# Delta attention and a PReLU feed-forward layer on one core: issuing loads of the first weight behind the first chunk's chain of small products

## The chip, the cores and the metric

The kernel runs on one core of one Trainium2 chip. The metric is the device time of one execution in microseconds (us), lower is better. The core has a matrix engine (TensorE, PE in the profile; PEld is its weight load), a vector engine (VectorE, DVE), a scalar engine (ScalarE, ACT), GpSimd (POOL) and SyncE (SP), which in this kernel issues nearly all transfers. Each engine works through its own list of instructions in order, and waits for other engines by semaphores.

## The reference

A gated delta-rule attention over 4 batches, 8 heads, 768 positions and head size 48, followed by a feed-forward layer from 384 to 2048 and back:

```python
for t in range(S):
    kt, vt, bt = (k_n[:, :, t], v[:, :, t], beta[:, :, t, None])
    y[:, :, t] = np.einsum('bhd,bhde->bhe', q[:, :, t], state)
    v_old = np.einsum('bhde,bhd->bhe', state, kt)
    state = state + bt[:, :, :, None] * np.einsum('bhd,bhe->bhde', kt, vt - v_old)
...
x = np.ascontiguousarray(attn_out.transpose(0, 2, 1, 3)).reshape(B * S, H * D)
...
h = x @ w_in
g = np.maximum(h, 0.0) + alpha * np.minimum(h, 0.0)
return (g @ w_out).astype(np.float32)
```

`k_n` is k divided by its norm. The feed-forward input has 3072 rows. The two weights are the reason for this case: they lie in memory as 64-bit numbers, and the kernel makes 32-bit numbers of them itself.

## The kernel before, in words

**Tiling.** The sequence is cut into 12 chunks of 64 positions, and the batch into two pairs, so there are 24 steps, `n` = 0 to 23. Steps 0 and 1 are the two pairs of chunk 0, steps 2 and 3 those of chunk 1, and so on. Within a chunk the recurrence is turned into a triangular system: its inverse is built by VectorE for blocks of 32 (`eliminate`, `eliminate_small`, `cross`), put together by many small products (`between_1`, `between_2`), applied to v (`solve`), and used for the output (`outputs`) and for the next state (`next_state`). `to_ffn` transposes the output of a step into `xt`, the input of the feed-forward layer. `ffn_in(c)` multiplies it with `w_in` (48 products for a chunk, six to a PSUM bank, two banks by turns), and ScalarE and VectorE empty a bank with one Relu (L913) and two VectorE instructions (L915).

**Order.** The order is written by hand; a generator is advanced for every instruction or two, and `weave` and `alongside` mix several generators in fixed proportions. What is written first goes first into each engine's list. Nothing is moved later by a scheduler.

**The weights.** `weights` returns three things: `fetch(n)`, which issues the loads up to the n-th piece on SyncE (L192); `begin(n)`, which does the first two of four conversion steps on ScalarE (L208, L209); and a generator `finish`, which does the other two on VectorE (L218, L223) and, after each piece, issues the loads of all further pieces whose staging buffer has come free (L227 to L230). `w_in` has 12 pieces of 512 KB each, numbered 0 to 11 here. There are `n_in` = 6 staging buffers, which lie in the space that `w_out` will take, so pieces 0 to 5 are loaded at the start, and piece 6 can be loaded only once piece 0 has been converted, piece 7 once piece 1 has, and so on. `ahead` says how far ScalarE's two steps may run ahead of VectorE's.

**Around the change.** `first_chunk` carries steps 0 and 1 through. While it runs, no other work is ready for TensorE, and so `busy` puts products without use between the small ones. `convert(2)` converts one piece, `convert(4)` two. The order in `first_chunk` is: piece 0; then `place`, `between_1` (L676), `between_2` (L695), `solve` (L762), `outputs` (L775), pieces 1 and 2, `next_state` (L791), pieces 3 and 4; then for both steps `to_ffn`, `load_late(i + 2)` and `load_v(i + 3)`; last, piece 5. `load_late` issues four loads of 48 KB on SyncE (L144) into a buffer that the `next_state` of the step two before has to be done with. `load_v` issues two loads of 96 KB (L120).

With piece 5 the generator calls `begin(7)`, so ScalarE's list holds the two steps of piece 6 right behind the copies of `to_ffn`. `second_pair` comes next: it starts chunk 1 and weaves into it the 48 products of `ffn_in(0)` and the conversion of pieces 6 to 11. In ScalarE's list stand there, in this order: piece 6, a square of k (L330), piece 7, the two copies of `cross` (L581), two copies of `flips` (L381, L383), a square, piece 8, and the first L913.

In SyncE's list before the change stand: the load of piece 6 (behind piece 0's conversion); the loads of pieces 7, 8, 9 and 10, each behind one conversion; the 12 loads of `load_late` and `load_v`; and the load of piece 11.

Of the kernel before, what the change touches and what calls it, by code (L numbers as in the profile page):

```python
# [41 lines left out]
def kernel(  # L42
# [34 lines left out]
    def ps_one():  # L77
        return ps_big()[:, 0]
# [4 lines left out]
    def ps_ffn():  # L83
        turn[0] ^= 1
        return ffn_banks[turn[0]]

    def half(i):
        return slice(64 * i, 64 * i + 64)
# [27 lines left out]
    def fetch(a, n, dst, queues=(nc.sync, nc.sync)):  # L116
        c, bp = steps[n]
        for t in range(2):
            src = a[2 * bp + t, :, c * C : (c + 1) * C, :].rearrange("h p d -> p h d")
            queues[t].dma_start(out=dst[half(t)], in_=src)  # L120
# [9 lines left out]
    def load_v(n):  # L130
        if n < N:
            v_raw[n] = work.tile([128, H, D], FP32, name="v_raw", bufs=3)
            fetch(v, n, v_raw[n])
# [26 lines left out]
    w_in = const.tile([128, KT, DFF], FP32, name="w_in")  # L160
    w_out = const.tile([128, FT, DM], FP32, name="w_out")

    ahead = [0]

    def weights(pieces, stages, ids, done):

        count = len(pieces)
        fetched, begun = [], []

        def words(i):
            w = stages[ids[i]]
            dst, src = pieces[i]  # L180
            shape = list(dst.shape)
            n = shape[1] * (shape[2] if len(shape) > 2 else 1)
            w = w[:, 0 : 2 * n]
            if len(shape) > 2:
                return w.rearrange("p (f e) -> p f e", f=shape[1]), n
            return w, n

        def fetch(n):
            while len(fetched) < min(n, count):
                i = len(fetched)  # L190
                assert ids[i] not in ids[len(done) : i]
                nc.sync.dma_start(out=words(i)[0], in_=pieces[i][1].bitcast(U32))  # L192
                fetched.append(i)

        def flat(x):
            return x.rearrange("p f d -> p (f d)") if len(x.shape) > 2 else x

        def halves(i):
            w = flat(words(i)[0]).rearrange("p (e w) -> p e w", w=2)
            return w[:, :, 0], w[:, :, 1], flat(pieces[i][0])  # L200

        def begin(n):
            while len(begun) < min(n, count):
                i = len(begun)
                assert i < len(fetched)
                lo, hi, dst = halves(i)

                nc.scalar.activation(dst.bitcast(U32), lo, ACT.Copy, scale=2.0**-29)  # L208
                nc.scalar.activation(  # L209
                    lo.bitcast(FP32), hi.bitcast(FP32), ACT.Prelu, scale=2.0**-112, alpha=-(2.0**32)  # L210
                )
                begun.append(i)

        def finish():
            for i in range(count):
                begin(min(i + 2, max(ahead[0], i + 1)))
                lo, _, dst = halves(i)
                nc.vector.tensor_scalar(  # L218
                    out=lo, in0=lo, scalar1=3, scalar2=None, op0=ALU.logical_shift_left
                )  # L220
                yield

                nc.vector.tensor_tensor(  # L223
                    out=dst.bitcast(U32), in0=lo, in1=dst.bitcast(U32), op=ALU.add
                )
                done.append(i)
                n = len(fetched)  # L227
                while n < count and ids[n] not in ids[i + 1 : n]:
                    n += 1
                    fetch(n)  # L230
                yield

        return fetch, begin, finish()

# [154 lines left out]
    def now(pieces):  # L391
        for x in pieces:
            x()
# [171 lines left out]
    def cross(m, bs, edge, half_way, aside=None):  # L565


        def let(b, every):
            if aside is not None and b % every == every - 1:
                aside()  # L570

        n = bs.stop - bs.start
        p = ps_one()[:, 0 : n * LB].rearrange("p (b i) -> p b i", i=LB)
        for b in range(n):
            for i in range(4):
                nc.tensor.matmul(
                    p[quad(i), b], edge[quad(i), bs.start + b],
                    turned[m][quad(i), bs.start + b, 0:LB],
                )
            let(b, 4)  # L580
        nc.scalar.copy(half_way[:, bs, 0:LB], p)  # L581
        yield
        p = ps_big()[:, :, 0 : n * LB].rearrange("p w (b i) -> p w b i", i=LB)
        for b in range(n):
            for i in (0, 2):
                nc.tensor.matmul(
                    p[quad(i), 1, b], inverse[m][quad(i), bs.start + b],
                    half_way[quad(i), bs.start + b, 0:LB],
                )
            let(b, 8)  # L590
        for b in range(n):
            for i in range(4):
                nc.tensor.matmul(
                    p[quad(i), 0, b], half_way[quad(i), bs.start + b],
                    inverse[m][quad(i), bs.start + b, LB:HB],
                )
            let(b, 4)
        for i in (0, 2):
            y = turned[m][quad(i), bs, 0:LB]
            nc.vector.tensor_tensor(out=y, in0=y, in1=p[quad(i), 1], op=ALU.add)  # L600
        y = inverse[m][:, bs, LB:HB]
        nc.vector.tensor_tensor(out=y, in0=y, in1=p[:, 0], op=ALU.add)
        yield
# [7 lines left out]
    def place(n, parts=(0, 1, 2, 3), by_vector=False):  # L611
        for _ in placing(n, parts, by_vector):
            pass
# [101 lines left out]
    def scale_v(n):  # L715
        if n < N and n not in nv:
            nv[n] = v_raw.pop(n)
            nc.vector.tensor_tensor(
                out=nv[n], in0=nv[n],
                in1=stats[n][0][:, :, None].to_broadcast([128, H, D]), op=ALU.mult,  # L720
            )
# [295 lines left out]
    in_done, out_done = [], []  # L1017
# [98 lines left out]
    def busy(n, p=None):  # L1116

        p = ps_one() if p is None else p
        while n > 0:
            x = p[:, 0 : int(512 * min(n, 1))]  # L1120
            nc.tensor.matmul(  # L1121
                x, ident[0:ROWS],
                k_t[NJ - 1].rearrange("p g i -> p (g i)")[0:ROWS, 0 : x.shape[-1]],
            )
            n -= 1
# [21 lines left out]
    def first_chunk(mask, convert):  # L1147

        both = (0, 1)
        ahead[0] = n_in  # L1150

        waits, pause = iter([0.5] * 2), []
        middle = cross(
            0, slice(0, 2 * H), edge, half_way, lambda: pause and busy(next(waits, 0), pause[0])
        )
        next(middle)
        pause.append(ps_one())
        busy(1, pause[0])
        begin_in(6)
        for i in both:  # L1160
            scale_v(i)
            mask(i)
        convert(2)
        next(middle)
        busy(1.25)
        place(0, (0,))
        place(1, (0,), True)
        for i in both:
            place(i, (1,), True)
            now(between_1(i))  # L1170
        busy(0.5, ps_ffn())
        for i in both:
            place(i, (2,))
            now(between_2(i))
        for i in both:
            now(through_state(i))
            now(solve(i))
        busy(0.5, ps_ffn())
        now(outputs(0))
        convert(4)  # L1180
        now(next_state(0))
        now(outputs(1))
        now(next_state(1))
        convert(4)
        busy(0.5, ps_ffn())
        for i in both:
            to_ffn(i, ps_ffn())
            load_late(i + 2)
            load_v(i + 3)
        ahead[0] = FT * DM  # L1190
        convert(2)

    def statics(first, last):
# [18 lines left out]
    pieces = [  # L1212
        (w_in[:, i, o : o + W_IN_P], moe_w_in[i * 128 : (i + 1) * 128, o : o + W_IN_P])
        for o in range(0, DFF, W_IN_P)
        for i in range(KT)
    ]
    n = 2 * W_IN_P
    n_in = FT * DM // n
    ids = [i % n_in for i in range(len(pieces))]
    fetch_in, begin_in, conv_in = weights(  # L1220
        pieces, [space[:, i * n : (i + 1) * n] for i in range(n_in)], ids, in_done
    )
    PARTS_IN = 2 * len(pieces)

    pieces = [(w_out[:, f], moe_w_out[f * 128 : (f + 1) * 128]) for f in range(FT)]
    stages = [space_out[:, i] for i in range(SPACES)]
    for f in range(FT // 2, FT, 2):
        stages.append(w_out[:, f : f + 2].rearrange("p f d -> p (f d)").bitcast(U32))
    ids = [0, 1, 2, 3, 4, 5, 6, 0, 1, 2, 6, 0, 1, 2, 0, 1]
    fetch_out, _, conv_out = weights(pieces, stages, ids, out_done)  # L1230
    PARTS_OUT = 2 * len(pieces)

    def chain(*gens):
# [35 lines left out]
    n = 12  # L1269

    def convert(n):
        for _ in part(conv_in, n):
            pass
# [218 lines left out]
```

## Time and profile before

| What | us |
|---|---|
| Time, median of 3 runs | 678.72 |
| Lowest and highest | 677.28, 832.73 |
| The profiled run | 677.22 |
| Span in the profile | 675.5 |

| Engine | Busy, us | Share |
|---|---|---|
| TensorE, products | 650.6 | 96% |
| TensorE, weight loads | 567.3 | 84% |
| VectorE | 452.1 | 67% |
| ScalarE | 271.4 | 40% |
| GpSimd | 35.9 | 5% |

The share of TensorE is that of the whole span. The change lies in the first 60 us of it, which have other limits: there the slices of the page show TensorE, VectorE, ScalarE and the transfers all far from a steady state. So the table tells only that time lost or gained by TensorE in the early part is not made up later by a large reserve; what the change does has to be read from the stretch from 34 to 70 us.

The transfers of that stretch are of three kinds: pieces of the weights (512 KB in packets of 4096 bytes), q, k and v (48 or 96 KB in packets of 192 bytes), and TensorE's own instructions, which the page lists as q8 "instruction": 74 packets, 1.21 MB in all.

### The profile page before, as it was taken

What the parts mean: (1) busy time and instruction counts of PE and PEld (TensorE: products, weight loads), DVE (VectorE), ACT (ScalarE), POOL (GpSimd) and SP (SyncE); (2) the same over time, 40 slices, a digit from 0 to 9 for tenths busy, and PEclk for the clock granted to TensorE, in tenths of its full rate; (3) what the DMA queues carried; (4) which work ended last, traced back from release to release, by engine and by line L of the source; (5) the groups of instructions that cost most, each with busy time, mean ns of one, the idle gap of its engine ahead of it and who ended that gap; (6) DMA issues with size and microseconds to landing.
All of it is one profiled execution on the core that took longest, in us unless ns stands there. A gap on an engine that the chain in (4) does not pass through costs nothing.

```text
span 675.5 us, 21591 instructions
## 1 busy us (share of the span) xinstructions
PE 650.6 (96%) x9359; PEld 567.3 (84%) x9359; DVE 452.1 (67%) x1125; ACT 271.4 (40%) x643; POOL 35.9 (5%) x105
## 2 busy tenths in 40 slices
PE   5999988999998999999999999999999999999997
PEld 4578877656587998998998998988989989989997
DVE  4946878878989869758859748859655355354261
ACT  4927746335556343344343343343244144021110
POOL 6000111101010000001000000000000000000000
PEclk9979999999999999999999999999999999999999
DMA  8838844211332022122112111111121110100000
GB/s 121 239 77 231 207 104 118 71 30 31 70 76 48 14 61 49 25 49 50 25 37 36 27 37 37 26 40 33 25 47 27 36 37 2 34 4 2 24 1 24
DMA packets 110959, 37.69 MB, mean 56 GB/s; under 512 B 104160, under 2 KB 107248, under 8 KB 110864
## 3 DMA queue, kind: packets, MB, share of 16 engines
q1 hardware_dynamic: 109088, 35.81, 24.5%
q8 instruction: 74, 1.21, 0.7%
q10 hardware_dynamic: 1776, 0.49, 0.4%
q14 instruction: 21, 0.17, 0.1%
HBM read 31.56 MB, written 4.72 MB: 54 GB/s over the span
## 4 chain that ended last, share of the span: by engine, by line
PE 76%; DVE 14%; ACT 5%; issue 2%; DMA 1%; SPq 1%; POOL 0%; ACTq 0%; DVEq 0%; POOLq 0%
PE p_ffn L903 30%; PE p_ffn L967 28%; DVE prod L499 2%; DVE block L505 2%; PE p_big L360 2%; PE p_big L762 2%; PE p_big L732 2%; PE p_big L775 2%; DVE act L915 2%; PE p_big L1121 2%; ACT diag L631 1%; PE p_big L407 1%; PE p_big L737 1%; PE p_big L791 1%; DVE block L472 1%
## 5 line engine op out<-in xcount | busy, mean ns | idle before, releaser
L903 PE MATMUL p_ffn<-xt,w_in 128*128 128x256 f32 x1152 | 261.6, 382 | 6.9 <-ACT sums L913 1.8
L903 PEld LDWEIGHTS p_ffn<-xt,w_in 128*128 128x128 f32 x1152 | 214.4, 190 | 38.6 <-issue 4.2
L915 DVE SCALAR_TENSOR_TENSOR act<-act,al_t,p_ffn 128x256 f32<-128x256 f32 x176 | 76.5, 476 | 81.0 <-ACT act L913 80.9
L913 ACT ACTIVATE act<-p_ffn 128x512 f32<-128x512 f32 x88 | 52.4, 595 | 144.8 <-PE p_ffn L903 144.6
L967 PE MATMUL p_ffn<-w_out,act 128*128 128x192 f32 x480 | 82.4, 328 | 0.1
L967 PEld LDWEIGHTS p_ffn<-w_out,act 128*128 128x128 f32 x480 | 77.6, 190 | 1.0 <-issue 0.5
L505 DVE TENSOR_TENSOR block<-block,prod 128x30 f32<-128x30 f32 (+9 forms) x150 | 49.9, 333 | 5.1
L499 DVE TENSOR_TENSOR prod<-block 128x30 f32<-128x30 f32 (+9 forms) x150 | 48.9, 326 | 3.3 <-POOL block L489 1.6
L987 DVE TENSOR_TENSOR o_sb<-u,p_ffn 128x192 f32<-128x192 f32 x40 | 13.3, 353 | 50.3 <-PE p_ffn L967 41.9
L816 ACT COPY xt<-p_big 128x384 f32<-128x384 f32 x22 | 10.4, 477 | 74.2 <-PE p_big L814 74.2
L967 PE MATMUL p_ffn<-space_out,sums 128*128 128x192 f32 x160 | 29.4, 327 | 0.0
L967 PE MATMUL p_ffn<-more,sums 128*128 128x192 f32 x160 | 29.3, 326 | 0.0
L755 ACT COPY y<-p_big 128x384 f32<-128x384 f32 x22 | 10.4, 477 | 43.0 <-PE p_big L737 41.3
L967 PE MATMUL p_ffn<-w_out,sums 128*128 128x192 f32 x160 | 27.6, 326 | 0.0
L967 PEld LDWEIGHTS p_ffn<-more,sums 128*128 128x128 f32 x160 | 26.6, 190 | 0.0
L967 PEld LDWEIGHTS p_ffn<-space_out,sums 128*128 128x128 f32 x160 | 26.5, 190 | 0.1
L967 PEld LDWEIGHTS p_ffn<-w_out,sums 128*128 128x128 f32 x160 | 26.3, 190 | 0.0
L708 ACT COPY inv<-p_big 32x256 f32<-32x256 f32 x38 | 13.8, 363 | 29.7 <-DVE u L766 29.4
L631 ACT ACTIVATE diag<-inverse,which 64x128 f32<-64x128 f32 (+2 forms) x60 | 24.3, 405 | 2.3 <-DVE inverse L472 1.3
L747 DVE TENSOR_TENSOR r<-v_raw,p_big 64x192 f32<-64x192 f32 (+1 forms) x66 | 23.2, 352 | 1.0
L349 POOL TENSOR_TENSOR beta_t<-beta_t,rec 128x8 f32<-128x8 f32 x24 | 6.2, 259 | 291.9 <-DVE rec L347 271.6
L332 DVE TENSOR_REDUCE norm<-ksq 128x8 f32<-128x384 f32 x24 | 13.0, 546 | 13.0 <-ACT ksq L330 13.0
(161 smaller groups left out, 954.0 us busy)
## 6 DMA issues: line engine op xcount, KB each, us to landing
w_out<-in_moe_w_in_dram SPq DMA_DIRECT2D x12, 512.0 KB, 4.9
qp<-in_q_dram SPq DMA_DIRECT2D x48, 96.0 KB, 3.0
v_raw<-in_v_dram SPq DMA_DIRECT2D x48, 96.0 KB, 2.9
kl<-in_k_dram SPq DMA_DIRECT2D x96, 48.0 KB, 2.7
out_dram<-o_sb SPq DMA_DIRECT2D x92, 48.0 KB, 1.6
space_out<-in_moe_w_out_dram SPq DMA_DIRECT2D x11, 384.0 KB, 4.6
ke<-in_k_dram SPq DMA_DIRECT2D x43, 96.0 KB, 3.1
w_out<-in_moe_w_out_dram SPq DMA_DIRECT2D x5, 384.0 KB, 4.3
```

The lines of the kernel that those rows point to most:

```text
L360: nc.tensor.transpose(p[0:ROWS, g * 128 : (g + 1) * 128], src[:, 2 * g : 2 * g + 2].rearrange("p h d -> p (h d)")[:, 0:ROWS], ident,)
L499: nc.vector.tensor_tensor(out=prod, in0=r[:, 0:j, j : j + 1].to_broadcast([128, j, n]), in1=r[:, j : j + 1, j + 1 : HB].to_broadcast([128, ...
L505: nc.vector.tensor_tensor(out=r[:, 0:j, j + 1 : HB], in0=r[:, 0:j, j + 1 : HB], in1=prod, op=ALU.add)
L631: nc.scalar.mul(out, x, which[rows, i : i + 1])
L708: nc.scalar.copy(to[rows], p[rows])
L732: nc.tensor.matmul(p[half(t ^ a), a, g], k_t[n][dims(a), g, half(t)], beside[bp][dims(a), t, g])
L747: nc.vector.tensor_tensor(out=r[to, a], in0=v_in[to, a], in1=p[own, a, :, 0:D], op=ALU.subtract)
L762: nc.tensor.matmul(p[half(t ^ a), a, g], inv[n % NE][half(t), a * G + g], rhs_[n][half(t), a, g])
L903: nc.tensor.matmul(p_h[:, i], w_in[:, t, (f + i) * 128 : (f + i + 1) * 128], xt[:, t], start=(t == 0), stop=(t == KT - 1),)
L913: nc.scalar.activation(g, p_h, ACT.Relu, scale=-1.0)
L915: nc.vector.scalar_tensor_tensor(out=g[:, i], in0=g[:, i], scalar=al_t[:, f + i : f + i + 1], in1=p_h[:, i], op0=ALU.mult, op1=ALU.add,)
L967: nc.tensor.matmul(p, x(i), w(i), start=(i == 0), stop=(i == FP - 1))
```

## The change

A flag `hold` is set at the beginning of `first_chunk`. While it is set, the conversion of a piece no longer issues the load of the next one. The loop that issued them is made a function of its own, `follow`, which is called once behind the 12 loads of `load_late` and `load_v` and in front of piece 5's conversion. So pieces 6 to 10 are loaded then, one behind the other, and piece 11 after piece 5 as before. The arithmetic, the buffers and the order on every engine except SyncE stay as they were. The aim is that the loads of `w_in` don't run beside the chain of small products.

```diff
-    ahead = [0]
+    ahead, hold = [0], [False]
...
                 done.append(i)
-                n = len(fetched)
-                while n < count and ids[n] not in ids[i + 1 : n]:
-                    n += 1
-                    fetch(n)
+                if not hold[0]:
+                    follow()
                 yield
...
-        return fetch, begin, finish()
+        def follow():
+            n = len(fetched)
+            while n < count and ids[n] not in ids[len(done) : n]:
+                n += 1
+                fetch(n)
+
+        return fetch, begin, finish(), follow
...
         ahead[0] = n_in
+        hold[0] = True
...
             to_ffn(i, ps_ffn())
             load_late(i + 2)
             load_v(i + 3)
+        hold[0] = False
+        follow_in()
         ahead[0] = FT * DM
         convert(2)
...
-    fetch_in, begin_in, conv_in = weights(
+    fetch_in, begin_in, conv_in, follow_in = weights(
...
-    fetch_out, _, conv_out = weights(pieces, stages, ids, out_done)
+    fetch_out, _, conv_out, _ = weights(pieces, stages, ids, out_done)
```

## The prediction

> **What bounds the kernel now.** I read the page first, then the chain of waits in order of time around the change, then a table of short stretches for the granted clock, then the lists of SyncE and ScalarE in order of time.
>
> The page says 96% for TensorE over the span. Nothing of the change touches TensorE's work, so the question is where TensorE waits or runs slowly near the change. The chain of waits from 36 to 58 us (start, duration, what):
>
> ```profile
> 36.74 1.11 PE p_big L676 x30
> 37.85 0.80 issue
> 38.65 1.25 PE p_big L676 x34
> 39.90 1.15 PE p_ffn L1121 x2
> 41.05 3.45 PE p_big L695 x62
> ...
> 44.60 1.73 PE p_big L762 x62
> 46.34 0.81 PE p_ffn L1121 x2
> ...
> 55.52 2.16 PE p_ffn L903 x10
> 57.68 0.33 PE p_big L586 x14
> ```
>
> TensorE itself carries the first chunk. Two things are odd: a stop of 0.80 us in the midst of L676 for which no engine is to blame, and L695, whose 64 products take 3.5 us, where 32 of them take 1.12 us in chunk 1. The table of stretches (the last three columns are granted clock, transfers' share, GB/s) tells why:
>
> ```profile
> 38.00:39.00 1.00, 0.35 (x10) 0.35 (x11) 0.00 (x0) 0.01 (x1) 0.00 (x0) 1.00 0.46 184
> 39.00:40.00 1.00, 1.00 (x32) 0.96 (x29) 0.00 (x0) 0.42 (x2) 0.00 (x0) 0.92 0.11 29
> 40.00:41.00 1.00, 1.00 (x4) 0.35 (x4) 0.00 (x0) 1.00 (x3) 0.00 (x0) 0.50 0.00 0
> ...
> 46.00:47.00 1.00, 1.00 (x16) 0.65 (x9) 0.70 (x3) 0.00 (x0) 0.00 (x0) 0.67 0.00 0
> ```
>
> From 39.84 to 46.67 the clock is half. The reader is also to see the zeros at the right: no transfer runs in these slow microseconds. Of the loads that the change moves, only piece 6 lies beside the chain. SyncE's list shows it, and then the others:
>
> ```profile
> 34.98 17.57 SPq L192 DMA_DIRECT2D w_out<-in_moe_w_in_dram  x5
> 52.65 2.65 SPq L144 DMA_DIRECT2D kl<-in_k_dram  x4
> 55.35 1.84 SPq L120 DMA_DIRECT2D v_raw<-in_v_dram  x2
> 57.29 2.63 SPq L144 DMA_DIRECT2D kl<-in_k_dram  x4
> 59.98 1.61 SPq L120 DMA_DIRECT2D v_raw<-in_v_dram  x2
> 61.71 0.54 SPq L192 DMA_DIRECT2D w_out<-in_moe_w_in_dram  x1
> ```
>
> The five in the first line, looked at singly, start at 34.98, 48.10, 49.17, 51.16 and 52.23. Last, who uses them. ScalarE's list (idle before an instruction in brackets) has piece 6 at 50.90, piece 7 at 52.62 and the two copies (L581) on which TensorE's L586 depends behind both:
>
> ```profile
> 50.90 0.69 ACT L208 ACTIVATE w_in<-w_out 128x512 uint32<-128x512 uint32 x1
> 51.62 0.69 ACT L209 ACTIVATE w_out<-w_out 128x512 f32<-128x512 f32 x1
> ...
> 52.62 0.69 ACT L208 ACTIVATE w_in<-w_out 128x512 uint32<-128x512 uint32 x1
> 53.34 0.70 ACT L209 ACTIVATE w_out<-w_out 128x512 f32<-128x512 f32 x1
> 53.92 0.25 ACT L581 COPY act<-p_big 128x128 f32<-128x128 f32 x1
> 54.62 0.27 ACT L581 COPY act<-p_big 128x128 f32<-128x128 f32 x1 [0.45 <-PE p_big L576]
> ```
>
> So ScalarE starts piece 6 as soon as the copies of `to_ffn` are through.
>
> [...] So a load behind a waiting load waits too; SyncE's 12.5 us wait for piece 1's conversion ahead of 48.10 agrees.
>
> **The change part by part.**
>
> *Piece 6 leaves the chain.* Its packets of 4096 bytes run from 36.30 to 39.6. [...] until 36.3 the transfers are packets of 192 bytes of q, issued from 31.78 to 34.88, which stay. So piece 6 can lengthen only what lies between the block's last byte and TensorE's going on: 36.86 to 38.65, 1.8 us. At the two other stops of this kind (85.95 and 89.74) that gap was 1.46 and 1.25 us. With 1.25 the stop shrinks from 0.80 to 0.25; bounds 0 and 0.8. I take 0.25. Then L676 ends at 39.2[...]. From 36.3 to 39.2 there are 2.9 us without a dense product[...], where before there were 3.5. So the dip probably goes, though not surely: other windows (101.3 to 104.7) keep the full clock with 1.8 us idle and 1.6 us of dense products, but no trace shows where the limit lies.
>
> *What the dip costs.* At full clock: L676 to 39.2, L1121 0.63 to 39.8, L695 64 products as 2 x 1.1 to 42.05, L703 0.42 and the second half of L762 0.54 with the latencies to 43.15, L1121 0.63 to 43.8. Before, L775 began at 47.07. Gain 3.3 us if the dip goes, about 0.5 if it stays.
>
> *Pieces 7 to 10 and piece 6 go behind 12 loads.* The first of the 12 needs `next_state(0)`, whose products end at 48.2 before, 44.9 with the gain. The page's and the lists' price of an issue is 0.65 us (2.65 for 4, 1.29 for 2): 12 make 7.8. So piece 6 is issued at 44.9 + 7.8 = 52.7. From issue to landing the pieces took 4.4 to 5.5, median 4.5 in this stretch: 57.2. Piece 7 comes 1.5 us later (512 KB at 340 GB/s), and so on. Their issue costs SyncE nothing that counts; the k and v loads now come some 4 to 5 us earlier, and nobody waits for them.
>
> *The wait that this adds.* ScalarE would start piece 6 at 50.9 - 3.3 = 47.6; now it stands until 57.2, 9.6 us. Queued behind it are the square, piece 7, L581, L381, L383, a square, piece 8 and the first L913. TensorE can do without them all up to L586: two groups of six `ffn_in` products fill two banks, of which nine products are reached, and `cross` and `flips` have buffers. It reaches L586 at 57.68 - 3.3 = 54.4. ScalarE: 57.2, pieces 6 and 7 2.8, square 0.45, first L581 0.25: 60.75. TensorE waits 6.3 us there. Against before, L586 comes at 60.8 instead of 57.7, 3.1 later.
>
> *What follows.* ScalarE has L581, L381, L383, square and piece 8 to do before L913: 0.25 + 0.5 + 0.48 + 0.42 + 1.3 gives 63.7, L913 0.55, L915 twice 0.87: 65.1. Only then may the last of the next four products use its bank; it ends at 65.35, where before they ended at 61.5: 3.8 later. [...] the clock halves once more. Until it comes back (two windows, 6.8 us, going by the first dip) TensorE loses up to 3.4, of which most lies beside ScalarE's catching up; I take 1. Sum: -3.3 + 7.1 + 1.0 = 4.8 us slower. From 58 to 90 us TensorE is busy over 90% of the time, so this isn't given back; ScalarE's idle pieces there (1.09, 1.69, 1.48, 1.11) let it catch up, not TensorE.
>
> **The rivals.**
>
> *A, the dip stays.* [...] Then +7.1 + 1.0 - 0.5 = 7.6: 685.6.
>
> *B, faster: the loads are hidden anyway.* For it: before, ScalarE waits only 0.4 us for a load anywhere from 10 to 130 us, by the list of waits, ScalarE is busy 40% only, and pieces may land sooner with no other loads in flight. Against: the list puts piece 6 behind 7.8 us of issues, and ScalarE takes it first. If ScalarE's wait cost TensorE nothing, 678 - 3.3 = 674.7; over 2% faster isn't reached even so, and would need something that no view shows.
>
> *C, the delay grows:* the issues take 8.9 us as before, landing takes 9.7 (the longest of `w_in`)[...], and the clock stays half for longer. 10 + 4 us: 692 or more. Nothing in the trace makes all of it likely.
>
> **How the numbers follow.** The base is 678 (677.28 and 678.72 of three runs; 832.73 is out of line). Forecast, dip gone and the wait paid: 678 + 4.8, about 682.8; chance 0.42. A: 685.6, 0.30. B: 674.7, 0.16, of which 0.03 for over 2% faster. C: 0.12. Two per cent is 13.6 us, so the forecast and A and nearly all of B are within it: faster 0.03, same 0.85, slower 0.12. The range from 676 to 690 takes in the forecast with the bounds of its costs, A, and half of B; what is left out is C and the lower half of B, about 0.2.
>
> **What would show it.** In the profile after: no load of 512 KB between 35 and 52 us; the 12 small loads from about 45; piece 6 issued near 53. The granted clock 1.00 from 40 to 47, L695 in about 2.2 us, the stop in L676 under 0.4: right on the gain; a half clock there means A. ScalarE idle for 8 us or more ahead of L208, released by a transfer, and TensorE idle for 5 us or more ahead of L586, with a dip behind it: right on the wait. If ScalarE's idle time there is under 3 us, or TensorE isn't held at L586, the main step is wrong.

## The result, and the profile after

The changed kernel takes 682.87 us (median of 6 runs, 681.88 to 685.04) against 677.68 for the kernel before (median of 6). The ratio is 1.0092, with an interval of 1.0063 to 1.0122: slower by 0.9%. One of the 6 runs of before, of 832.73 us, lies far above the other five (674.53 to 678.72) and says nothing of the kernel. On another occasion the same kernel came to 687.94 against 675.32, ratio 1.0171 (1.0135 to 1.0207). The experiment g1_change_again below takes up why the two differ.

The chain of waits of the changed kernel, from the first small products to the point where TensorE goes on with chunk 1 (start, duration, what; L680, L699, L766, L779 and L590 are L676, L695, L762, L775 and L586 of before):

```profile
37.50 2.24 PE p_big L680 x64
39.74 0.63 PE p_ffn L1125 x2
40.37 1.93 PE p_big L699 x62
...
45.31 0.34 PE p_big L779 x23
45.66 0.75 issue
46.41 0.37 PE p_big L779 x9
...
55.35 5.96 DMA w_out<-in_moe_w_in_dram
...
61.70 0.28 ACT act L585
61.98 0.04 issue
62.02 0.97 PE p_big L590 x29
```

In this execution the stop in the first product group is gone, L699 takes 1.93 us where L695 took 3.45, and the chain from L680 to the first L779 lasts 6.7 us instead of 10.4. A stop of 0.75 us stands further on, in L779, where before had none in this stretch. And the chain then runs through a transfer for 6 us, which it didn't before. SyncE's list tells which:

```profile
45.33 2.64 SPq L144 DMA_DIRECT2D kl<-in_k_dram  x4
48.05 1.61 SPq L120 DMA_DIRECT2D v_raw<-in_v_dram  x2
49.76 2.63 SPq L144 DMA_DIRECT2D kl<-in_k_dram  x4
52.48 1.27 SPq L120 DMA_DIRECT2D v_raw<-in_v_dram  x2
53.85 3.91 SPq L192 DMA_DIRECT2D w_out<-in_moe_w_in_dram  x6
```

The 12 small loads take the queue from 45.33 to 53.75, and the refill follows. ScalarE's list (idle time and its releaser in brackets), and TensorE's longest wait:

```profile
48.24 0.86 ACT L820 COPY xt<-p_ffn 128x384 f32<-128x384 f32 x2 [0.95 <-PE p_ffn L818]
58.80 0.66 ACT L208 ACTIVATE w_in<-w_out 128x512 uint32<-128x512 uint32 x1 [9.70 <-DMA w_out<-in_moe_w_in_dram]
```

```profile
PE p_big L590 <- ACT act L585: 6.3, 1, 6.3
```

ScalarE stands for 9.70 us ahead of piece 6; TensorE, which has other work until 55.7, stands for 6.3. The short stretches (third number from the right: granted clock) show that the clock falls in TensorE's wait and stays low after it:

```profile
56.00:57.00 1.00, 0.00 (x0) 0.00 (x0) 0.00 (x0) 0.00 (x0) 0.00 (x0) 1.00 0.82 229
60.00:61.00 1.00, 0.00 (x0) 0.00 (x0) 0.41 (x1) 1.00 (x3) 0.00 (x0) 0.50 0.99 406
69.00:70.00 1.00, 1.00 (x66) 0.86 (x66) 0.42 (x2) 0.85 (x4) 0.00 (x0) 0.81 0.67 67
```

From 59.13 to 69.37 the clock is half, 10.24 us, and TensorE works again from 62.02.

### The profile page after: what moved, and what is told of

It is laid out like the page before. It is cut to its first block, busy times and chain, and to the rows that moved or that the text cites. A ratio compares the mean times of both kernels' runs of the same rounds, so it can differ in the third digit from the quotient of the medians.

```text
span 680.4 us, 21594 instructions
## 1 busy us (share of the span) xinstructions
PE 651.7 (96%) x9359; PEld 567.6 (83%) x9359; DVE 452.0 (66%) x1125; ACT 271.3 (40%) x643; POOL 35.7 (5%) x105
## 4 chain that ended last, share of the span: by engine, by line
PE 78%; DVE 12%; ACT 5%; DMA 2%; issue 1%; SPq 1%; ACTq 0%; POOL 0%; DVEq 0%; POOLq 0%
PE p_ffn L907 31%; PE p_ffn L971 27%; PE p_big L364 2%; DVE prod L503 2%; PE p_big L736 2%; DVE block L509 2%; PE p_big L779 2%; PE p_big L766 2%; PE p_big L1125 2%; PE p_big L411 2%; DVE act L919 1%; PE p_big L741 1%; PE p_big L795 1%; DMA ke<-in_k_dram 1%; DVE block L476 1%
## 5 line engine op out<-in xcount | busy, mean ns | idle before, releaser
L820 ACT COPY xt<-p_big 128x384 f32<-128x384 f32 x22 | 10.4, 477 | 74.2 <-PE p_big L818 74.2
L759 ACT COPY y<-p_big 128x384 f32<-128x384 f32 x22 | 10.4, 476 | 43.0 <-PE p_big L741 41.4
L635 ACT ACTIVATE diag<-inverse,which 64x128 f32<-64x128 f32 (+2 forms) x60 | 24.3, 405 | 2.3 <-DVE inverse L476 1.3
```

Source lines behind the costliest of these rows:

```text
L635: nc.scalar.mul(out, x, which[rows, i : i + 1])
```

## The experiments

Each run gives, beside its time, its mean granted clock; (1 - clock) x span x 2 is the time at half clock. The trace of before records 17.07 us at full clock, 6.83 at half and 628.05 at full, that of the change 34.13, 10.24 and 610.99; these are 5, 2, 184, 10, 3 and 179 times 3.413 us. Only a rest at half clock at the very end (0.8 us in before, under 0.1 in the change) is shorter. I call 3.41 us a window. I use this below: the median of a kernel mixes executions with different numbers of windows, so I give the least time too; the least of 22 runs is not quite on a par with that of 6. The kernels of the first group share 58 runs of the kernel before, with median 675.22.

**The refill released early: e1_behind_solve.** In the changed kernel:

```diff
             now(solve(i))
+        load_v(3)
+        hold[0] = False
+        follow_in()
         busy(0.5, ps_ffn())
...
             load_late(i + 2)
-            load_v(i + 3)
-        hold[0] = False
-        follow_in()
+            if i > 0:
+                load_v(i + 3)
```

> The changed kernel, but the refill is released behind the solve of steps 0 and 1 instead of behind the whole chain, with load_v(3) in front of it, whose wait for solve(0) is what keeps piece 6 back; the other ten small loads come behind pieces 6 to 10. My theory (gain by the clock, loss by ScalarE's wait for piece 6): piece 6 is issued at about 43.7 us and has landed by 48.3, before ScalarE reaches it at about 49; the clock stays full from 40 to 47; TensorE isn't held at the second phase of cross (0 instead of 6.3 us) and doesn't go cold. Time about 674.5, 3 under before (677.7) and 8 under the change. Rival 1 (the clock dip is a matter of chance, the loads have nothing to do with it): same as before, 677 to 678. Rival 2 (the change is slow for another reason than ScalarE's wait): stays near 682.

Measured: 676.09 (least 674.00), ratio to before 1.0007 (0.9987 to 1.0027). Its ScalarE list where the change has the wait of 9.70 us:

```profile
49.42 0.71 ACT L208 ACTIVATE w_in<-w_out 128x512 uint32<-128x512 uint32 x1 [0.29 <-DMA w_out<-in_moe_w_in_dram]
```

No wait but these 0.29 us, no stop of TensorE at L590, and a mean clock of 0.999 in the profiled execution. Up to the last transposes of `to_ffn` it runs as the change does: its 900th product record starts at 48.30, that of the change at 48.26. At the 1200th they are at 61.41 and 69.72, 8.3 us apart, and at the 9300th at 660.88 and 666.95. So the loss of the change arises here, and in this pair of executions 6.1 of it stays. Rival 2 falls. But the other half of the expectation fell too: with piece 6 out of the way of most of the chain, the kernel is no faster than the kernel before, as rival 1 had it. The 677.7 that I had taken for before was no good centre; its 58 runs here have 675.22.

**The clock alone: e2_dense_in_gap.** In the kernel before:

```diff
-        busy(1.25)
+        busy(1.75)
...
             now(between_1(i))
+            if i == 0:
+                busy(0.25, ps_ffn())
```

> The kernel before, with piece 6 beside the chain as it was, and two more useless dense products: busy(1.25) ahead of between_1 becomes busy(1.75), which fills TensorE's wait for the first diagonal blocks, and a busy(0.25) stands between between_1 of step 0 and of step 1. My theory (the half clock, not the transfer itself, is what the chain loses, and the transfer acts only through the stop it lengthens): full clock from 40 to 47, L695 in about 2.2 us, L676 to L775 some 3 us shorter less 0.3 us for the added products: about 675, though piece 6 still lies beside the chain. Rival (the transfer itself slows the small products): L695 and L762 stay at 3.5 and 1.8 us, time 678 or a little more.

Measured: 676.26 (least 673.61), ratio 1.0012 (0.9987 to 1.0037). In the profiled execution piece 6 lies beside the chain and the clock is full all through (span 672.6):

```profile
40.00:41.00 1.00, 1.00 (x20) 0.67 (x20) 0.00 (x0) 1.00 (x3) 0.00 (x0) 1.00 0.00 0
43.00:44.00 1.00, 0.91 (x35) 0.85 (x34) 0.72 (x3) 0.00 (x0) 0.00 (x0) 1.00 0.00 0
```

```profile
40.57 1.93 PE p_big L695 x62
```

So the transfer beside them doesn't slow the small products here: L695 takes 1.93 us, as L699 does in the change. The rival falls. But the gain of 3 us didn't come, and 6 of 22 runs are without a half-clock window, where before has 27 of 95 over all occasions. The added products changed nothing that can be seen in how often the clock falls.

**ScalarE's order: e3_scalar_later.** In the changed kernel piece 6 is begun later (the pieces left out are woven into three later groups):

```diff
-        ahead[0] = FT * DM
         convert(2)
...
-        alongside(4, 2)
+        weave((part(first_in, 4), 4))
...
-        alongside(5, 2)
+        weave((part(first_in, 5), 5))
+        ahead[0] = FT * DM
         next(halves[0])
```

> The changed kernel with SyncE's order as it is; only the conversion of pieces 6 to 11 starts later: piece 6 isn't begun in first_chunk, and the first two groups of products in second_pair have no pieces woven in (the pieces go to the later groups). My theory: the loss of the change is the place of piece 6 in ScalarE's list ahead of the two copies of cross. With these copies ahead of it TensorE's stop at the second phase of cross goes from 6.3 us to under 1, there is no cold clock from 59 to 69, and the time is about 675 (before, less 3, plus up to 1 for a denser conversion later). Rival (the late landing itself costs, wherever ScalarE takes the piece, because the conversion is what bounds the next stretch): 680 to 683.

Measured: 681.79 (least 678.99), ratio 1.0091 (1.0064 to 1.0118). The stop at L590 is gone, as expected; the time is not 675 but in the rival's range. ScalarE's waits of this kernel from 50 to 72 us:

```profile
ACT w_in L208 <- DMA w_out<-in_moe_w_in_dram: 2.9, 1, 2.9
ACT act L585 <- PE p_big L580: 2.8, 2, 2.3
```

It still waits 2.9 us for piece 6 and has pieces 6 and 7 (2.7 us) ahead of the next bank and of the copies (L635) on which L680 hangs. TensorE now stands there, and the clock is half all the same, from 64.89 to 75.13:

```profile
70.24 1.80 PE L680 MATMUL p_big<-diag,right 64*64 64x32 f32 x29 [1.90 <-ACT diag L635]
```

```profile
69.00:70.00 1.00, 0.00 (x0) 0.00 (x0) 0.95 (x6) 0.32 (x1) 0.00 (x0) 0.50 1.05 420
```

So by the median the rival is right: the late landing costs, wherever ScalarE takes the piece, and the stop at L590 is only one of the places where TensorE can pay for it. In the least time taking the piece later saves 2.9 us (678.99 of 21 runs against 681.88 of the first six of the change). The profiled execution shows one thing more. The small loads and pieces 6 to 10 are ordered as in the change, nothing lies beside the chain, and yet:

```profile
42.00:43.00 1.00, 1.00 (x25) 1.00 (x22) 0.25 (x1) 0.00 (x0) 0.00 (x0) 0.50 0.00 0
```

The clock is half here at 42 us and, by another row, at 46 (0.50 in both), and L699 takes 2.96 us where the change has 1.93. Keeping piece 6 away did not prevent that.

**The cold stretch: e4_warm_wait and g2_warm_early.** Both add about 5 us of dense products without use to the changed kernel. The first puts `busy(6, spare[-1])` in front of the second phase of `cross`, into the unused bank of its PSUM tile.

> The changed kernel with about 5.2 us of useless dense products at the place where TensorE stands for 6.3 us ahead of the second phase of cross; they write an unused PSUM bank and the wait stays as it is. My theory: the wait costs twice, once as such and once because TensorE comes out of it at half clock (in the changed kernel 2.9 us of lag between the first and the second half of cross of steps 2 and 3). With the products the clock stays full from 59 to 69, and the time is 682.9 less 3: about 680. Rival (ScalarE's catching up, not the clock, sets that stretch): 682 to 683, with the clock full all the same.

Measured: 690.01, ratio 1.0217 (1.0171 to 1.0264). It tests nothing, because the products came after the wait instead of in it: they waited for the copies of the other bank of the same tile.

```profile
PE p_big L1129 <- ACT act L589: 8.0, 1, 8.0
```

The second puts them in front of those copies:

```diff
+        busy(fill, both_banks[:, 1])
         nc.scalar.copy(half_way[:, bs, 0:LB], p)
```

> The changed kernel with 5.2 us of useless dense products right behind the first phase of cross for step 3, in front of the copy that ScalarE makes of it, so that TensorE does them while ScalarE waits for piece 6 (in e4_warm_wait they came behind the copies, after the wait). My theory: TensorE reaches the second phase of cross at about 61 instead of 55.7, still before the copies (62.0); the clock is full from 59 to 69; the least time falls by the 2.9 us of the cold stretch, from 681.9 to 679, and many runs show a clock over 0.995. Rival (ScalarE's catching up sets that stretch, not the clock): full clock, same time, 682 to 683.

Measured: 683.67 (least 681.33), ratio 1.0120 (1.0090 to 1.0150). TensorE works until 60.8 and waits 1.5 us. The clock, in three of the stretches:

```profile
63.00:64.00 1.00, 1.00 (x71) 0.97 (x59) 0.12 (x1) 1.00 (x3) 0.00 (x0) 1.00 1.02 418
66.00:67.00 1.00, 0.32 (x2) 0.30 (x2) 1.00 (x3) 0.91 (x4) 0.00 (x0) 1.00 1.07 419
69.00:70.00 1.00, 1.00 (x42) 0.96 (x35) 0.06 (x1) 1.00 (x3) 0.00 (x0) 0.50 1.40 131
```

From the first to the second half of `cross` TensorE needs 5.0 us (62.33 to 67.36), in the change 7.2 (62.02 to 69.21), in the kernel before 3.8. Of the 3.4 us, I thus estimate 2.2 for the cold clock and 1.2 for ScalarE's catching up. But they weren't saved singly: TensorE now waits for ScalarE at 66, where it is busy for 0.32 us of 1, the clock is half at 69 (0.50), and the first product group of chunk 1 (L680 of the change) starts at 72.77, in the change at 72.46. The rival is right about the time, my theory about the clock in this stretch. The division rests on one execution of each kernel.

**How much must be ahead: g3_six_loads_ahead and h1_four_loads_ahead.** The refill is released in the loop at the end of `first_chunk`, in the first with

```diff
             load_v(i + 3)
-        hold[0] = False
-        follow_in()
+            if i == 0:
+                hold[0] = False
+                follow_in()
```

and in the second with the same lines between `load_late` and `load_v`.

> The changed kernel with the refill released in the middle of the 12 small loads: load_late(2) and load_v(3), six loads, stand ahead of pieces 6 to 10, the other six behind. My theory: piece 6 lands six issues of 0.7 us, some 4.5 us, earlier (about 54 instead of 58.7), ScalarE waits about 5 us instead of 9.7, TensorE at the second phase of cross about 1.5 to 2 instead of 6.3[...]: least time 675 to 676, median about 677. Rival (any late refill costs the same, or the small loads have nothing to do with it): 682 to 683.

Measured: 683.33 (least 678.48), ratio 1.0101 (1.0058 to 1.0143). The median is in the rival's range, the least time between the two.

> The changed kernel with only load_late(2), four loads of 48 KB, in front of pieces 6 to 10, and the other eight small loads behind them. With two loads ahead (e1_behind_solve) TensorE's stop was 0, with six 4.5, with twelve 6.3 to 7.1 us. My theory (the cost is the landing of piece 6 against the place where ScalarE takes it, less what TensorE can do meanwhile): issue at about 48.0, piece 6 on hand at about 53, ScalarE waits about 4 us, TensorE 0.5 to 1.5 us at the second phase of cross[...]. Least time 674.5 to 676.5, median 677 to 679. Rival (once the refill waits for the end of the chain the full price is due, however few loads are ahead): least time 681, median 683.

Measured: 678.22 (least 675.44), ratio 1.0056 (1.0031 to 1.0082) against 27 runs of before on the same occasion, with median 674.93. TensorE's wait for the copies of `cross` in the two profiles:

```profile
PE p_big L590 <- ACT act L585: 4.5, 1, 4.5
```

```profile
PE p_big L590 <- ACT act L585: 2.3, 1, 2.3
```

Both stops are longer than I said, and the clock, which I had estimated to stay full, is half (0.50) behind both, at 61 us in g3 and at 59 us in h1:

```profile
61.00:62.00 1.00, 1.00 (x67) 1.00 (x66) 0.00 (x0) 1.00 (x3) 0.00 (x0) 0.50 1.38 158
```

```profile
59.00:60.00 1.00, 1.00 (x16) 0.96 (x9) 0.89 (x2) 0.97 (x3) 0.00 (x0) 0.50 0.37 62
```

In h1 piece 7 is late as well, for a reason that was not tested; ScalarE waits for both pieces:

```profile
52.33 0.68 ACT L208 ACTIVATE w_in<-w_out 128x512 uint32<-128x512 uint32 x1 [3.54 <-DMA w_out<-in_moe_w_in_dram]
55.99 0.66 ACT L208 ACTIVATE w_in<-w_out 128x512 uint32<-128x512 uint32 x1 [1.88 <-DMA w_out<-in_moe_w_in_dram]
```

Taken together they show the cause:

| Small loads ahead of the refill | ScalarE's first wait, us | TensorE's stop, us | Least time, us | Median, us (runs) |
|---|---|---|---|---|
| 2 (e1) | 0.3 | 0 | 674.00 | 676.09 (22) |
| 4 (h1) | 3.5 | 2.3 | 675.44 | 678.22 (22) |
| 6 (g3) | 6.6 | 4.5 | 678.48 | 683.33 (6) |
| 12 (the change) | 9.7 | 6.3 | 681.88 | 683.46 (12, with g1 below) |

All four hold the refill out of the chain up to `solve` or longer. h1, g3 and the change differ only in the number of issues ahead; e1 releases the refill earlier as well. Both waits and the least time rise with that number. The medians don't separate six from twelve: four of the six runs of g3 have four windows or more at half clock. The rival, that the full price is due as soon as the refill waits for the end of the chain, falls with h1.

**One part alone: g4_only_first_beside.** `hold` is set only after piece 0's conversion, so that piece 6 is loaded beside the chain as before, and pieces 7 to 10 are held.

> One part of the change alone: piece 6 is loaded beside the chain as in the kernel before, and only pieces 7 to 10 are held until the 12 small loads are issued. My theory: the cost is the wait of ScalarE for whichever piece comes first behind the 12 loads; ScalarE does piece 6 and a square, then stands for piece 7, which lands at about 58.8 as piece 6 did; the copies of cross follow 2 us sooner than in the change (piece 6 is out of the way), so TensorE waits about 4.3 us instead of 6.3; least time 679.5 to 680, median about 681. Rival (piece 6 alone matters, since it alone lay beside the chain): as before, 675.

Measured: 682.75 (least 681.54), ratio 1.0117 (1.0084 to 1.0151).

```profile
59.31 0.66 ACT L208 ACTIVATE w_in<-w_out 128x512 uint32<-128x512 uint32 x1 [9.05 <-DMA w_out<-in_moe_w_in_dram]
```

It costs nearly what the whole change costs. Whichever piece is the first behind the 12 loads makes ScalarE stand. TensorE's stop is 5.6, not 4.3: piece 7, now the first of the refill, is on hand at 59.3, no sooner than piece 6 was in the change (58.8), and the copies of `cross` follow at 60.55 instead of 61.70. In the least time it makes 0.3 us. So piece 6 beside the chain or behind it is worth next to nothing; the rival falls.

**The change once more: g1_change_again.**

> The changed kernel as it is, once more, for the spread of its times and of its mean granted clock. The runs of the kernel before and of the first experiments show that a half clock in the first chunk comes and goes from run to run (18 of 58 runs of before have none at all). If the change removes that dip, as the prediction had it, nearly all runs show a mean clock of 0.992 (three windows of 3.41 us, those behind ScalarE's wait). If the dip is chance and has nothing to do with the loads, some half of the runs show more than three windows, as before shows more than none; the median is then some 7 to 8.5 us above before's median, near 683, and the gain that the prediction counted (3.3 us) doesn't exist.

Measured: 687.94, ratio 1.0171 (1.0135 to 1.0207). In its profile ScalarE stands for 10.49 us ahead of piece 6 and TensorE for 7.1. By the mean clocks, two runs have 3 windows at half clock and four have 9 or 10; of the first six runs four have 3 and two have 5. So the two ratios differ by the runs with many such windows, and because before came to 677.68 on the first occasion and to 675.32 here. All twelve together have a median of 683.46, and the six with only the three windows behind ScalarE's wait have 682.72. The kernel before has 95 runs with a known clock on the three later occasions, median 675.20: 27 have no window at all (median 673.57), 47 have two or more. In the change 6 of 12 have two or more beyond the three. Twelve runs are few, and only a trace tells where the windows lie; but nothing here shows that the change makes them rarer.

## Why the prediction was right, and where it was not

The time said was 682.8, the median 682.87. That closeness is partly luck: two terms were off, in opposite directions.

*The wait that is added: right.* Of the predicted working, piece 6 was to be issued at 52.7 (measured 53.85), ScalarE to stand 9.6 us (9.70), TensorE 6.3 at the second phase of `cross` (6.3), and L590 to start at 60.8 (62.02; this execution was 0.8 late from the start). e1, h1 and g4, and g3 in its least time, show that ScalarE's wait for the first piece behind the small loads, and not another part of the change, is the loss; e3 shows that it isn't the stop at L590 alone. The 12 issues took 8.4 us, not 7.8.

*What follows: too small.* TensorE's lag was to grow by 0.7 us for ScalarE's catching up and by 1 for the cold clock, with L586 for step 3 as the mark; from the profiles of the change and of g2 I estimate 1.2 and 2.2 there. That the clock would fall in TensorE's stop was an estimate; it did, at 59.13, and the half clock lasted 10.24 us, not 6.8. The prediction had it that none of the lag is given back; some of it is: between the change and e1, which run alike up to 48.3, the lag falls from 8.3 to 6.1 by the end.

*The gain of 3.3 us: this step failed.* "So the dip probably goes" was an estimate, read from one execution of the kernel before, which happened to have the dip, and the profile of the change happened not to. With no piece beside the first product groups, the 62 products of L699 (L695 of before) take 1.93 us in the change, e1, g1, g2 and h1, their time at full clock in e2 (1.00 at 40 us), and 2.96 in e3 and 3.45 in g3 and in e4 (L703); with piece 6 beside them they take 3.45 in before, at half clock, and 1.93 in e2 and g4. And e1, where piece 6 was out of the way and nothing was lost, is no faster than before. The size was too large as well: runs of before with two windows at half clock lie 1.6 us above those with none.

The reasoning on the stop in L676 was no better. The block it speaks of is the q8 packet of 16.4 KB that moves from 35.98 to 36.86 in before; TensorE goes on 1.79 us after its last byte, and that the stop waits for this packet was an estimate. The 0.80 us is one draw: the stop is 0.23 and 0.34 us in e2 and g4, which have piece 6 beside it, and 0.17 to 0.43 in e1, e3, g1, g2, g3 and h1, which don't; in the change it is missing. So the forecast of 0.25 was near, but nothing here shows that the transfer of piece 6 makes the difference. The stop in L779 is another one, which the prediction didn't count: it is there with piece 6 beside the chain too, 1.12 us in e2 and 0.54 in g4.

What makes the clock fall was not shown. In the 3.41 us ahead of the dip of before, 36.43 to 39.84, TensorE was busy for 2.30 us, mostly with the 64 small products of L676; in e3 and g3 it stopped in the same group for 0.43 and 0.33 us, and the clock fell too; in the change, where that group has no stop, and in e1, g1, g2 and h1, where the stop is 0.17 to 0.41 us, it did not. In e4 TensorE has no wait in the chain from 33.98 to 38.65, and L684 (L676 of before) takes 3.56 us for its 64 products, where L680 in the change, without a stop as well, takes 2.24. The second dip of the change lies differently: TensorE stood from 55.7 to 62.0, and the clock fell at 59.13.

*The base: wrong by nearly as much.* The 678 contained time at half clock (6.83 us from 39.84 on in the profiled run). Against the 675.2 of 95 runs, the change costs 683.46 - 675.20 = 8.3 us, not 4.8; without a gain, the prediction's own 7.1 + 1.0 for the wait and what follows make 8.1. That is rival A's arithmetic (7.6: the wait is paid and next to nothing is gained), and A was the right case in substance, although the forecast named the time. The two occasions by themselves give 5.2 and 12.6 us between the medians, so the 8.3 is rough. Rival B falls: the loads are not hidden. C isn't reached by the medians, 692 or more; the longest of the twelve runs is 688.45.

## What to carry to other kernels

Before a transfer is moved back in a queue that issues in order, add up the issues that then stand ahead of it and compare its landing with the moment at which its consumer takes it; here 12 loads of at most 96 KB cost 8.4 us of queue, and ScalarE's own list passed the delay on to TensorE and VectorE, which stood for 6.3 and 9.5 us. If transfers must be held, hold the ones that nobody is waiting for: with the same refill ahead of ten of the twelve small loads the loss is gone (e1, ratio 1.0007). And read an odd clock or a short stop in one profile as one execution: look at the clocks of many runs before a gain is counted on its going away.

## What the runs showed of the hardware that was not expected

- The mean clock of a run resolves single windows, since in before and the change the times at half clock come as multiples of 3.41 us (6.83 and 10.24) but for the end of the run. Over the 58 runs of before that the first group shares, each microsecond at half clock costs about 0.28 us. The runs of the kernel before with exactly two windows have a median 1.6 us above those with none (675.20 against 673.57).
- In TensorE's stop of 6.3 us in the change (55.7 to 62.0) the clock fell, at 59.13, and it was half until 69.37, with TensorE at work again from 62.02; the same work in g2, with a stop of 1.5 us, still had the full clock at 66 (1.00) and had half at 69 (0.50).
- A stop in L779 (L775 in the kernels without the change) is in the change, e1, g1, g2 and h1 (about 0.75 us), in g4 (0.54) and in e2 (1.12), with little or nothing on the transfer engines in the change (shares of 0.00 to 0.17). It is missing in before, e3, e4 and g3, whose 62 products of L695 (L699, in e4 L703) took 2.96 to 3.45 us shortly before, instead of 1.93. In the change the last q8 packet of 16.4 KB ahead of it ends at 45.00, and TensorE goes on at 46.41, 1.41 us later. No run shows what TensorE waits for there.
